# A new order of all steps, and products of zeros over 128 and over 64 rows, in a kernel of decay attention and mixture-of-experts attention

## The chip, the cores and the metric

The kernel runs on one core of a Trainium2 chip. The metric is the time of one execution on the device in microseconds (us), from the start of the program to its end; the median of three runs is given. The engines of the core are TensorE (PE; its loading of weights is shown apart as PEld), VectorE (DVE), ScalarE (ACT), GpSimd (POOL) and SyncE (SP), which here issues the transfers (DMA). Tiles in PSUM are where PE writes its products.

## The reference

There are 8 batches, 8 heads, 576 positions and a head dimension of 64. A causal attention with a decay comes first; its output, 512 columns wide, is the input of an attention with 4 experts, of which a gate picks two for each position.

```python
scores = scale * np.matmul(q, k.transpose(0, 1, 3, 2))
cum = np.cumsum(np.log(np.clip(f, 0.0001, 1.0)), axis=-1)
scores = np.where(causal, -1000000000.0, scores + cum[:, :, :, None] - cum[:, :, None, :])
attn = np.exp(scores - np.max(scores, axis=-1, keepdims=True))
x = np.matmul(attn / (np.sum(attn, axis=-1, keepdims=True) + 1e-09), v)
...
logits = x @ w_gate
topk = np.argpartition(-logits, 2, axis=-1)[..., :2]
w = softmax of the two chosen logits
for e in range(E):
    q, k, v = x @ wq[e], x @ wk[e], x @ wv[e]
    a = causal softmax of scale * (q @ k.transpose(0, 2, 1))
    out += (w of e, or zero where e is not chosen) * (a @ v @ wo[e])
```

## The kernel before

The work is cut into units of two heads: four for each batch in the first attention (a0_0 is batch 0, heads 0 and 1) and two of two experts each in the second (m0_0). A unit goes through a row of steps, each a Python generator that yields after nearly every instruction:

- prep_attn (L369) has SP fetch queries and keys into xin, ACT rounds them into kq (L377, twice: keys, queries), DVE subtracts to get the rest ka (L383, twice), and SP copies the bits of each into the other tile (L367). Rows with the running sums of the logarithms of the decay (chl) come into kq by way of a DRAM tile ex (L292 to L304, L363), for the first unit straight from chl (L359).
- max_pass (L532) has PE make products m0 to m3 in PSUM (L541), DVE adds the mask and takes maxima of them (mxs at L547, mxt at L560), PE turns the maxima around (mp, L604), ACT negates them (ms, L607), and SP writes them into a row of kq (L367), so that the products that follow have the maximum subtracted already. m and mp tiles share a pool of two tiles in PSUM.
- scores (L629) makes the products s0 to s3 (L638, L639); ACT takes their exponentials P, POOL clears what lies above the diagonal (L625, L658) and adds up rows (R, L701 to L707). attend (L713) multiplies by the values va (oa, ob, L726).
- For the experts, moe_front (L400) makes the values and the logits of a batch (pv, L417, in five blocks), copies the logits out (lg, L436) and works out the gate on DVE (L443 to L475: comparisons g and t of 128x80, wins, the largest logit mx, gt) with one exponential on ACT (L464). prep_moe (L497) makes queries and keys of the experts (pp, L513, twelve products for a tile), ACT rounds them (L521), DVE subtracts (ka_m, L523). project_out (L847) multiplies by wo and sends the output.

The order of all this is a table: ORDER (L27) is a string of two-digit numbers to base 64, each the number of a task, and each entry moves that task on by one yield. After that every instruction of an engine is made to follow the one written before it on the same engine (L920 to L925), so the order on each engine is fixed by the table; nothing overtakes, and an instruction that waits holds up all behind it on its engine.

PE begins with products of zeros: a tile wz of zeros (L179), multiplied with itself into a tile of PSUM that nobody reads. warm(8) at L271 issues eight at the front. In prep_attn of the first three units two more are issued with each of ACT's conversions (L379) and one with each of DVE's subtractions (L385), and each is made to wait for the instruction it is issued with.

## Time and profile before

| | |
|---|---|
| runs | 747.75, 748.61, 749.22 us; median 748.61 |
| profiled execution | 747.97 us, of which 746.2 are the span of the profile |
| mean clock granted to PE | 0.975 of full speed |
| PE, DVE, POOL, ACT busy | 694.5, 587.7, 453.6, 445.9 us |
| PE's share of the chain that ended last | 64%; DVE 21%, ACT 4%, issue 3%, DMA 3%, POOL 3% |

The page cuts the span into 40 slices of 18.7 us and gives for each the busy share of an engine and the clock that PE was granted, in tenths. PE runs at one of two clocks, 2.4 or 1.2 GHz, which the page shows as 1.0 and 0.5. A row of the timeline is one instruction or a run of like ones, with its start, its duration and, in brackets, how long the engine stood idle before it and on whose work it waited. Products overlap, so a row's duration is longer than the step to the next row. The profile times one execution; its clock records begin at 13.27 us, and the slice before shows full speed without one.

### The profile page before, as it was taken

The page shows a single profiled execution, that of the slowest core. Times are in us where ns is not written, and L with a number is a line of the kernel's source. Part 1 is how long each engine was busy: PE and PEld are TensorE (multiplying, and loading weights), DVE is VectorE, ACT ScalarE, POOL GpSimd, SP SyncE. Part 2 cuts the span into 40 slices and gives each one's busy share as a digit, 9 for nine tenths or more (in the row PEclk, how much of TensorE's full clock was granted, in tenths as well). Part 3 has the DMA queues.
Part 4 walks back from the last instruction along what each step waited for, and adds up shares of the span by engine and source line. Part 5 has one row for each costly group of instructions (what it writes and reads, how often), then busy time and mean ns, then how long its engine had stood idle before and what let it go on. Part 6 is the DMA issues. An engine that isn't in the chain of part 4 may idle for free.

```text
span 746.2 us, 15368 instructions
## 1 busy us (share of the span) xinstructions
PE 694.5 (93%) x5346; PEld 557.8 (75%) x5346; DVE 587.7 (79%) x1666; ACT 445.9 (60%) x959; POOL 453.6 (61%) x767
## 2 busy tenths in 40 slices
PE   5788899989999989999899999999899999999987
PEld 1455687768787778878797787878688777879754
DVE  7578987988879788888789788788978898765732
ACT  3566655666477655686466664766466664655443
POOL 8788774685475863673656745765645864535350
PEclk9599999999999999999999999999999999999989
DMA  7776333432324244345243426353252442213103
GB/s 166 187 162 149 92 87 82 124 81 64 104 74 126 67 101 118 96 123 120 63 120 96 114 52 145 87 139 89 61 136 68 129 94 52 52 49 76 32 5 124
DMA packets 29470, 72.82 MB, mean 98 GB/s; under 512 B 4169, under 2 KB 4649, under 8 KB 27345
## 3 DMA queue, kind: packets, MB, share of 16 engines
q1 hardware_dynamic: 29393, 71.84, 38.9%
q8 instruction: 42, 0.69, 0.4%
q14 instruction: 35, 0.29, 0.1%
HBM read 32.91 MB, written 10.35 MB: 58 GB/s over the span
## 4 chain that ended last, share of the span: by engine, by line
PE 64%; DVE 21%; ACT 4%; issue 3%; DMA 3%; POOL 3%; SPq 0%; DVEq 0%; ACTq 0%
PE pp_m L513 11%; PE pv L417 7%; PE s_a L638 6%; PE m_a L541 5%; PE po L859 5%; PE s_a L639 5%; PE ob_a L726 5%; DVE ka_a L383 4%; DVE junk_a L547 4%; PE s_m L638 3%; PE m_m L541 3%; PE s_m L639 3%; PE sm_a L766 2%; PE ob_m L726 2%; PE oa_a L726 2%
## 5 line engine op out<-in xcount | busy, mean ns | idle before, releaser
L547 DVE CUSTOM_DVE_ANT_0 junk_a<-m_a,mask 128x320 bf16<-128x320 f32 (+2 forms) x192 | 93.5, 487 | 29.3 <-PE m_a L541 19.3
L638 PE MATMUL s_a<-ka_a 128*128 128x320 f32 (+4 forms) x384 | 111.8, 315 | 1.9 <-ACT P_a L655 1.2
L541 PE MATMUL m_a<-kq 128*128 128x320 f32 (+4 forms) x384 | 95.9, 326 | 18.8 <-DVE mxs_a L547 8.3
L639 PE MATMUL s_a<-kq 128*128 128x320 f32 (+4 forms) x384 | 104.6, 300 | 1.2 <-DMA kq<-ms_a 1.1
L383 DVE TENSOR_TENSOR ka_a<-xin,kq 64x1152 fp32r<-64x1152 f32 x64 | 98.1, 1533 | 2.7 <-ACT kq L377 1.3
L625 POOL TENSOR_SCALAR_AFFINE_SELECT P_a<-P_a 128x128 f32<-128x128 f32 x128 | 39.6, 312 | 94.4 <-ACT P_a L673 51.9
L521 ACT ACTIVATE kq<-pp_m 64x288 fp32r<-64x288 f32 x128 | 51.8, 405 | 67.0 <-DVE ka_m L523 42.3
L541 PEld LDWEIGHTS m_a<-kq 128*128 128x128 f32 (+1 forms) x384 | 64.0, 188 | 35.5 <-DVE mxs_a L547 16.2
L523 DVE TENSOR_TENSOR ka_m<-pp_m,kq 64x288 fp32r<-64x288 f32 x128 | 58.2, 454 | 38.9 <-ACT kq L521 36.4
L638 PEld LDWEIGHTS s_a<-ka_a 128*128 128x128 f32 (+1 forms) x384 | 71.0, 185 | 13.5 <-ACT P_a L655 3.8
L377 ACT ACTIVATE kq<-xin 64x1152 fp32r<-64x1152 f32 x64 | 72.5, 1157 | 8.9 <-DMA xin<-in_qk_dram 8.1
L701 POOL TENSOR_TENSOR R_a<-P_a 128x448 f32<-128x448 f32 x64 | 76.8, 1200 | 0.0
L658 POOL TENSOR_SCALAR_AFFINE_SELECT P_a<-P_a 128x256 f32<-128x256 f32 x64 | 31.8, 503 | 70.0 <-ACT P_a L655 69.7
L639 PEld LDWEIGHTS s_a<-kq 128*128 128x128 f32 (+1 forms) x384 | 70.5, 185 | 2.6 <-DMA kq<-ms_a 1.9
L726 PE MATMUL ob_a<-P_a,va 128*64 128x320 f32 (+1 forms) x512 | 67.7, 407 | 0.0
L703 POOL TENSOR_TENSOR R_a<-R_a,P_a 128x320 f32<-128x320 f32 x64 | 65.0, 1016 | 4.3
L638 PE MATMUL s_m<-ka_m 128*128 128x192 f32 (+2 forms) x192 | 56.0, 315 | 2.0 <-ACT P_m L655 1.6
L547 DVE CUSTOM_DVE_ANT_0 junk_m<-m_m,mask 128x192 bf16<-128x192 f32 (+2 forms) x96 | 46.6, 485 | 10.9 <-PE m_m L541 7.0
L726 PEld LDWEIGHTS ob_a<-P_a,va 128*64 128x64 f32 x512 | 35.9, 138 | 24.1 <-issue 0.2
L655 ACT ACTIVATE P_a<-s_a 128x512 f32<-128x512 f32 x64 | 37.2, 596 | 25.9 <-PE s_a L639 24.9
L639 PE MATMUL s_m<-kq 128*128 128x192 f32 (+2 forms) x192 | 52.2, 299 | 0.4 <-DMA kq<-ms_m 0.3
L673 ACT ACTIVATE P_a<-s_a 128x448 f32<-128x448 f32 x64 | 34.5, 545 | 25.6 <-PE s_a L639 25.0
(189 smaller groups left out, 2057.2 us busy)
## 6 DMA issues: line engine op xcount, KB each, us to landing
xin<-in_qk_dram SPq DMA_DIRECT2D x32, 576.0 KB
ka_a<-kq SPq DMA_DIRECT2D x64, 288.0 KB
va<-in_v_dram SPq DMA_DIRECT2D x32, 320.0 KB
ka_m<-kq SPq DMA_DIRECT2D x32, 288.0 KB
out_dram<-outb SPq DMA_DIRECT2D x32, 256.0 KB
kq<-ex SPq DMA_DIRECT2D x47, 27.0 KB
kq<-ms_a SPq DMA_DIRECT2D x64, 2.5 KB
out_dram<-outb SPq DMA_DIRECT2D x8, 128.0 KB
```

The source lines that it names most:

```text
L377: made = nc.scalar.activation(hi[near], x[:, 2 * c : 2 * c + 2], AF.Copy)
L383: made = nc.vector.tensor_tensor(lo, x[:, 2 * c : 2 * c + 2], hi[near].bitcast(F32), ALU.subtract)
L417: nc.tensor.matmul(pv[:, :NV], l[c][:, t0 : t0 + 128], r[:, c], start=(n == 0), stop=(n == 3 * KC - 1))
L513: nc.tensor.matmul(pp[:, :HS], w[:, c, es], x[c][:, gs], start=(n == 0), stop=(n == 3 * KC - 1))
L523: nc.vector.tensor_tensor(lo[:, h, gs], src, hv.bitcast(F32), ALU.subtract)
L541: nc.tensor.matmul(dst, qB[0:K, h, i0 : i0 + dst.shape[0]], kB[0:K, h, j0:j1], start=True, stop=True)
L547: nc.vector.tensor_tensor_reduce(jk[:, :n], src, mask[:, MW - n :], 1.0, init, ALU.add, ALU.max, acc)
L638: nc.tensor.matmul(dst, kaf[:, c : c + m], qA[:, h, i0:i1], start=True, stop=False)
L639: nc.tensor.matmul(dst, kqf[0:K, c + h * S : c + h * S + m], qB[0:K, h, i0:i1], start=False, stop=True)
L701: g.tensor_tensor(r[:, h, 128:S], q[:, 320:768], q[:, 768:1216], ALU.add)
L703: g.tensor_tensor(r[:, h, 256:S], r[:, h, 256:S], q[:, 1216:1536], ALU.add)
L726: mm = nc.tensor.matmul(dst[64 * h : 64 * h + 64, c0 : c0 + rhs.shape[-1]], vs[h][0:kp, blk], rhs, start=first, stop=last,)
```

## The change

The zeros change in kind. wz is now float32 of 128x512 in place of bfloat16, its memset accordingly twice as large, and there are two tiles of PSUM for the products. warm(at, cols, ...) issues one product for each start row in `at`: (0,) is one over all 128 rows (or over the lower 64), (0, 64) a pair of products over 64 rows each, into the two tiles. At the front there are 3 over 128 rows, 4 pairs, 3 over the lower half, 6 pairs of only 128 columns, and three times one over 128 rows and a pair: 23 products of 512 columns and 12 of 128, where there were 8. In the first three units a conversion has a pair with it (before: two products), a subtraction one product (as before).

ORDER is written anew from the first row to the last; its rows tell a reader nothing, so the diff shows one of each. Every instruction but the zeros is the same in kind and number.

```diff
 ORDER = """
-4w004w4w4w4w054x4z4x00004w4w000000004x4x4x4x02024x4y4y4y0202020202020202054x4x02020202024x4x4x4x4x4x4x4x4x074x0c
...
+4w4w4w4z004z02054x4w4w4w4y00004x4x00000000000202024x4x4x4x024x0202024y4y0505004y0c020202074x024y02024x4x4x054x4x
...
 """
 WARM = (1, 1, 1)
-WARM0 = 8
 
 
 @with_exitstack
@@ -176,14 +175,15 @@
     NKQ = 4
     kqs = [const.tile([128, 2, 2, S], F32R, name=f"kq{i}") for i in range(NKQ)]
     xin = const.tile([128, 4, S], F32, name="xin")
-    wz = const.tile([128, 512], BF16, name="wz")
-    nc.vector.memset(wz, 0.0)
-    wps = ptile(ps_o, "o", "warm")
-
-    def warm(n, after=None):
-
-        for _ in range(n):
-            mm = nc.tensor.matmul(wps, wz[:, 0:128], wz, start=True, stop=True)
+    wz = const.tile([128, 512], F32R, name="wz")
+    nc.vector.memset(wz.bitcast(F32), 0.0)
+    wps = [ptile(ps_o, "o", f"warm{i}") for i in range(2)]
+
+    def warm(at, cols, after=None, n=None):
+
+        for i, r in enumerate(at):
+            k = slice(r, r + (n or 128 // len(at)))
+            mm = nc.tensor.matmul(wps[i][:, :cols], wz[k, 0:128], wz[k, :cols], start=True, stop=True)
             if after is not None:
                 together(mm, after)
 
@@ -268,7 +268,10 @@
     neg = rows.tile([128, 2, S], F32, tag="R", name="neg")[:NR]
     nc.vector.memset(neg, -1.0)
 
-    warm(WARM0)
+    full, halves_, low_half = ((0,), 512), ((0, 64), 512), ((0,), 512, None, 64)
+    thin = ((0, 64), 128)
+    for args in 3 * [full] + 4 * [halves_] + 3 * [low_half] + 6 * [thin] + 3 * [full, halves_]:
+        warm(*args)
 
     def decay_rows():
         cum = prob.tile([128, 2, 1536], F32, tag="P", name="cum")[:NR, 0, :S]
@@ -376,13 +379,15 @@
         for c, hi in ((1, kB), (0, qB)):
             made = nc.scalar.activation(hi[near], x[:, 2 * c : 2 * c + 2], AF.Copy)
             if u["first"] is not None:
-                warm(2 * WARM[u["first"]], made)
+                for _ in range(WARM[u["first"]]):
+                    warm((0, 64), 512, made)
             yield
         yield from extra_rows(u, b * NPH + hp)
         for c, hi, lo in ((1, kB, kA[far]), (0, qB, qA[near])):
             made = nc.vector.tensor_tensor(lo, x[:, 2 * c : 2 * c + 2], hi[near].bitcast(F32), ALU.subtract)
             if u["first"] is not None:
-                warm(WARM[u["first"]], made)
+                for _ in range(WARM[u["first"]]):
+                    warm((0,), 512, made)
             yield
         copy_bits(kA[near], kB[near])
         yield
```

What moves is shown at three places, by the rows of an engine in the order of the program (a number at the end of a name is the number of the tile; three dots mark rows left out; line numbers of the changed kernel are up to five higher).

SP's queue at its start, before. xin is the transfer of queries and keys of a unit (the third is that of a0_2), chl the decay rows, ka_a0_0 the rest of the first unit's queries and keys:

```order
L374 DMA xin_112<-in_qk_dram 64x2304 x2
L337 DMA st_v0_152<-in_wv_dram 128x512
L359 DMA kq0_108<-chl_122 2x1x576 x2
L292 DMA ex_119<-chl_122 64x2x576
L294 DMA ex_119<-neg_126 64x2x576
L296 DMA ex_119<-one_123 64x1152
L374 DMA xin_112<-in_qk_dram 64x2304
...
L367 DMA ka_a0_0_138<-kq0_108 64x2x576
...
L367 DMA ka_a0_0_138<-kq0_108 64x2x576
```

And SP's queue at the same place, changed:

```order
L340 DMA st_v0_170<-in_wv_dram 128x512
L377 DMA xin_112<-in_qk_dram 64x2304 x2
L295 DMA ex_120<-chl_123 64x2x576
L362 DMA kq0_108<-chl_123 2x1x576 x2
L370 DMA ka_a0_0_172<-kq0_108 64x2x576
L297 DMA ex_120<-neg_127 64x2x576
L299 DMA ex_120<-one_124 64x1152
L370 DMA ka_a0_0_172<-kq0_108 64x2x576
L377 DMA xin_112<-in_qk_dram 64x2304
```

The write of chl to ex is now ahead of the two copies of chl into kq0, both copies of ka_a0_0 are ahead of the third xin, and the other weights, before between the third xin and ka_a0_0, follow later.

PE at the fifth gate, before, from the last product of pv5_4 (which holds the logits) to the second pair of m0 products of a6_3, for which PE waited; m0_a6_3, mp_a6_2 and m3_a6_2 share the pool of two tiles:

```order
L417 MATMUL pv5_4_7306<-vh_150,xl_a5_2_1_6947 128x260
L513 MATMUL pp_m5_0_7319<-xh_a5_2_0_6805,kh_273 128x288
...
L541 MATMUL m0_a6_3_7353<-kq1_109 128x192
L541 MATMUL m0_a6_3_7353<-kq1_109 128x320
L726 MATMUL oa_a6_1_7358<-P_a6_1_7189,va1_102 64x256 x2
...
L726 MATMUL ob_a6_1_7360<-pl2_107,va1_102 64x64 x2
L604 MATMUL mp_a6_2_7387<-ident_90,mxs_a6_2_7034 10x128
L513 MATMUL pp_m5_0_7407<-xh_a5_0_0_6485,kh_273 128x288
L513 MATMUL pp_m5_0_7407<-xl_a5_0_0_6486,kh_273 128x288
L513 MATMUL pp_m5_0_7407<-xh_a5_0_0_6485,kl_274 128x288
L541 MATMUL m0_a6_3_7411<-kq1_109 128x192
```

And PE at the same place, changed; between the rows shown there are 24 pp products in all and the two blocks of s3_a6_1:

```order
L422 MATMUL pv5_4_7320<-vh_168,xl_a5_2_1_6988 128x260
L546 MATMUL m3_a6_2_7337<-kq0_108 128x320
L518 MATMUL pp_m5_0_7348<-xh_a5_0_0_6495,kh_335 128x288
...
L643 MATMUL s3_a6_1_7369<-ka_a6_1_6526 128x320
...
L609 MATMUL mp_a6_2_7378<-ident_90,mxs_a6_2_7110 10x128
L546 MATMUL m0_a6_3_7409<-kq1_109 128x192
L518 MATMUL pp_m5_0_7416<-xh_a5_0_0_6495,kh_335 128x288
...
L731 MATMUL oa_a6_1_7430<-P_a6_1_7219,va1_102 64x256 x2
...
L546 MATMUL m0_a6_3_7449<-kq1_109 128x192
```

Before, 6 + 3 pp products, one pair of m0, the attend products (oa, ob) and mp stand between the last pv product and the second pair of m0. Now it is the last m3, 24 pp, s3, mp, one pair of m0 and the attend products, and mp stands ahead of the first m0 instead of between the two.

DVE at the fifth gate, before, with the last reduction of a6_2 (junk_a6_2) and the first of a6_3:

```order
L547 ISA junk_a6_2_7317,mxs_a6_2_7034<-m3_a6_2_7313,mask_95 128x320
L843 TENSOR_TENSOR yl_m4_0_1_7276<-ot_m4_1_6965,yh_m4_0_1_7275 128x512
L436 COPY lg5_7079<-pv5_4_7306 128x4
L443 TENSOR_TENSOR g45_7347<-lg5_7079 128x80
L445 TENSOR_TENSOR t45_7348<-lg5_7079 128x80
...
L462 TENSOR_TENSOR gt5_7382<-lg5_7079,mx5_7380 128x20
L547 ISA junk_a6_3_7384,mxs_a6_3_7350<-m0_a6_3_7353,mask_95 128x192
L560 TENSOR_REDUCE mxt_a6_3_7352<-m0_a6_3_7353 128x1
L523 TENSOR_TENSOR ka_m5_0_7218<-pp_m5_0_7319,kq2_110 64x288 x2
```

And DVE at the same place, changed:

```order
L441 COPY lg5_7096<-pv5_4_7320 128x4
L448 TENSOR_TENSOR g45_7341<-lg5_7096 128x80
L552 ISA junk_a6_2_7346,mxs_a6_2_7110<-m3_a6_2_7337,mask_95 128x320
L848 TENSOR_TENSOR yl_m4_0_1_7313<-ot_m4_1_7006,yh_m4_0_1_7312 128x512
L450 TENSOR_TENSOR t45_7342<-lg5_7096 128x80
...
L467 TENSOR_TENSOR gt5_7403<-lg5_7096,mx5_7401 128x20
L528 TENSOR_TENSOR ka_m5_0_7178<-pp_m5_0_7348,kq2_110 64x288 x2
L552 ISA junk_a6_3_7412,mxs_a6_3_7352<-m0_a6_3_7409,mask_95 128x192
```

The last reduction of a6_2 and the subtraction yl now stand inside the gate, and two ka_m subtractions between the gate and the first reduction of a6_3. PE and DVE are changed in a like manner at the gates of the other batches. On PE the m3 products of the first unit stand ahead of the zeros that are issued with the third unit's conversions, and on SP the load of va2 stands behind the maxima of a0_2 (kq2<-ms_a0_2), where it stood ahead.

## Rows read from the trace of the kernel before

**Rows 1.** the slices of the page: TensorE's granted clock, in tenths of full speed

```profile
PEclk9599999999999999999999999999999999999989
```

**Rows 2.** busy time by stretch: window, length, busy us (instructions) of each engine, clock

```profile
core 0: us, PE busy (x) PEld busy (x) DVE busy (x) ACT busy (x) POOL busy (x), PEclk, DMA share, GB/s
0.00:60.00 60.00, 42.15 (x189) 25.33 (x189) 40.94 (x92) 30.17 (x50) 48.40 (x76) 0.80 0.77 174
400.00:600.00 200.00, 193.18 (x1506) 158.38 (x1505) 166.98 (x476) 127.54 (x273) 127.28 (x213) 0.99 0.42 104
```

**Rows 3.** timeline of PE: start, us, what (count), in brackets idle time before it

```profile
1.26 3.59 PE L186 MATMUL warm<-wz 128*128 128x512 bf16 x8 [1.26 <-DVE wz L180]
9.33 2.52 PE L186 MATMUL warm<-wz 128*128 128x512 bf16 x5 [4.48 <-ACT kq L377]
```

**Rows 4.** timeline of DVE at the start

```profile
0.94 0.27 DVE L180 MEMSET wz<- 128x256 uint32 x1 [0.94 <-PEq L952]
23.44 0.49 DVE L547 CUSTOM_DVE_ANT_0 junk_a<-m_a,mask 128x320 bf16<-128x320 f32 x1 [2.92 <-PE m_a L541]
```

**Rows 5.** timeline of SP's queue, at its issues, over the first 56 us

```profile
10.51 0.68 SPq L292 DMA_DIRECT2D ex<-chl  x1
19.66 0.66 SPq L367 DMA_DIRECT2D ka_a<-kq  x1
21.50 0.82 SPq L367 DMA_DIRECT2D ka_a<-kq  x1
46.78 1.27 SPq L395 DMA_DIRECT2D va<-in_v_dram  x1
```

**Rows 6.** the chain that ended last: start, us, transfer

```profile
51.77 5.55 DMA kq<-ms_a
334.61 3.07 DMA kq<-ms_a
```

**Rows 7.** timeline of PE: what waits behind the gate of each batch

```profile
194.50 0.28 PE L604 MATMUL mp_a<-ident,mxs_a 128*10 128x128 f32 x1 [1.34 <-DVE mxs_a L547]
279.78 0.28 PE L604 MATMUL mp_a<-ident,mxs_a 128*10 128x128 f32 x1 [2.13 <-DVE mxs_a L547]
367.00 0.37 PE L513 MATMUL pp_m<-xh_a,qh 128*128 128x288 f32 x1 [2.16 <-DVE ka_m L523]
454.28 0.39 PE L541 MATMUL m_a<-kq 128*128 128x256 f32 x1 [0.90 <-DVE mxt_a L560]
538.17 0.52 PE L541 MATMUL m_a<-kq 128*128 128x192 f32 x2 [2.87 <-DVE mxt_a L560]
626.91 0.39 PE L541 MATMUL m_a<-kq 128*128 128x256 f32 x1 [1.46 <-DVE mxs_a L547]
```

**Rows 8.** busy time by stretch: two stretches behind a gate, columns as above

```profile
368.26:371.67 3.41, 3.41 (x16) 3.12 (x14) 1.74 (x6) 1.88 (x5) 0.12 (x1) 0.50 0.76 159
538.93:542.33 3.40, 3.40 (x17) 3.40 (x16) 2.38 (x9) 1.63 (x5) 0.00 (x0) 0.50 0.02 5
```

**Rows 9.** timeline of PE ahead of the wait at 538.17

```profile
530.52 0.28 PE L417 MATMUL pv<-vh,xl_a 128*128 128x260 f32 x1
530.63 0.29 PE L513 MATMUL pp_m<-xh_a,kh 128*128 128x288 f32 x1
531.77 0.87 PE L726 MATMUL oa_a<-P_a,va 128*64 128x256 f32 x8
```

**Rows 10.** timeline of DVE beside it, the fifth gate

```profile
530.76 1.99 DVE L843 TENSOR_TENSOR yl_m<-ot_m,yh_m 128x512 fp32r<-128x512 f32 x1
532.68 0.15 DVE L436 COPY lg<-pv 128x4 f32<-128x4 f32 x1
537.01 0.42 DVE L462 TENSOR_TENSOR gt<-lg,mx 128x20 f32<-128x20 f32 x1
```

**Rows 11.** PE's waits by line: for what, us, times, longest

```profile
PE m_a L541 <- DVE mxs_a L547: 8.3, 13, 1.5
```

**Rows 12.** one line of the gate: ns shortest, middle, longest, first and last start

```profile
L447 DVE TENSOR_TENSOR g<-g,up x8: 229/628/1580, 122.0 to 707.3; 128x80 f32<-128x80 f32 x8
```

188 lines of the change are left out of this document (94 added, 94 removed).

## The prediction

> **What bounds the kernel now.** I read the slices of the page first, then busy time by stretch, then what TensorE (PE) waited for, then the queue of SyncE (SP) and the other engines where a wait pointed at them. In the middle of the kernel PE is the bound: it is busy for 193.18 of the 200 us from 400 to 600, at a granted clock of 0.99 of full speed, while VectorE (DVE) has 166.98 and ScalarE and GpSimd less than 130 each [rows 2]. An order of work can win there only the idle 3.4%, and whatever time the clock is lowered. In the first 60 us PE is busy for 42.15 and so idle for 17.85, with a mean clock of 0.80 [rows 2]; the second slice of the span stands at half speed (a 5, the level of 1.2 GHz) [rows 1]. So there are two places to look at: the start, and the few large waits of the middle.
>
> The large waits of the middle stand where DVE works out the gate of the mixture of experts, once for each batch. In batches 1 to 6 there are six, at 194.50, 279.78, 367.00, 454.28, 538.17 and 626.91: 1.34 + 2.13 + 2.16 + 0.90 + 2.87 + 1.46 = 10.86 us in all [rows 7]. Two of them, those of 2.16 and 2.87, are followed by a stretch of 3.41 and 3.40 us in which the granted clock is 0.50, PE being busy throughout [rows 8]; what ran at half speed for 3.4 us takes 1.7 at full speed, so each of these stretches costs 1.7. The reader is to see that PE fell to the lower level right after it had stood still for over 2 us, and that the 2.13 us at 279.78 were not followed by such a stretch.
>
> **The zeros at the front.** PE first runs eight products of zeros in 3.59 us, 0.449 each, and then waits 4.48 us for the first conversion of the queries and keys [rows 3]. The changed kernel puts 16 such lengths there if the two products of a pair run beside each other, with six thin pairs of a quarter of the columns: 16 x 0.449 + 6 x 0.11 = 7.8 us; one after the other it is 23 lengths and 12 thin ones, 11.7 us. Before there was 3.59 + 4.48 = 8.07 us. The first fits into the wait and costs nothing; the second would push the zeros 3.6 us past it, of which the later products of zeros (they wait for ACT and DVE in any case) take up some. Bounds 0 and +3; I take 0, since a thing that fits into a wait of 4.48 us is the nearer row. No row of this trace has a product over 64 rows in two banks. The Trainium skill ("TensorEngine Tiling (Array Packing)", Key Properties) says that tiles work independently, so that pairs would run beside each other, but also that a change of the tiling mode, not merely of the tile, drains TensorE; that speaks against a list that alternates between full products and pairs. By the first half of it the sum is the one taken, by the second a drain is added at each of the dozen changes, and no run here gives its price.
>
> **The start behind them.** The memset of zeros is twice as large: 0.27 us [rows 4] becomes an estimated 0.54, and DVE's chain to the decay rows starts 0.27 later. On SP's queue the write of the decay rows to DRAM (0.68, [rows 5]) now stands ahead of the two copies that the first unit needs, and the two copies of ka_a0_0 stand ahead of the third transfer of xin. These two take 0.66 + 0.82 = 1.48 us of the queue [rows 5]. In the kernel before, what held the first unit up was that the second m3 product and the products behind it stood behind zeros tied to the third unit's conversion, which waited for that transfer of xin: DVE stood idle for 2.92 us until it came, at 23.44 [rows 4]. The m3 products are now ahead of these zeros, so the 2.92 go. What is late next is still the third xin, now 1.48 us later in its queue, since the conversion's zeros remain ahead of mp_a0_0. Net 2.92 - 1.48 = 1.44, and the copies of ka_a0_0, which the first scores need, are no longer behind the weights: I take -1.6. Bounds -2.9 (the later xin is hidden) and +1.5 (it is not, and the 2.92 comes back).
>
> A second place: the rows of maxima of a0_2 reached kq2 by a transfer that took 5.55 us on the chain, against 3.07 for the same transfer at 334.61 [rows 6]. Ahead of it in the queue stood the load of va2, 1.27 us of issue [rows 5]; this now stands behind. I take -1.3; bounds 0 and -2.5 (the difference of the two rows). The start is worth -2.9 in sum. That the half-speed stretch at the start goes as well is not counted; it would be worth up to 4 us, since the second slice of 18.7 us holds at most some 8 us of products that could run at double the speed [rows 1].
>
> **The gates.** Take the fifth. The last product of pv starts at 530.52 [rows 9]. Then PE has, before, six pp products and two m0 products (530.63 to 531.77: 1.14 us), and the attend products, mp and three pp (531.77 to the start of the wait at 538.17 - 2.87 = 535.30: 3.53 us): 4.67 us of work [rows 7, 9]. DVE in the same time finishes a subtraction of 1.99 us, starts the gate at 532.68 and ends its last operation at 537.43, 4.75 us later, and only then reduces m0, for which PE waits [rows 10]. In the changed order PE has behind the last pv product: one m3, 24 pp, two blocks of scores, mp, two m0 and the attend products. By the same rows a pp is 0.13 us, so this is 3.2 + 0.2 + 0.8 + 0.35 + 2.9 = about 7.4 us ahead of the second pair of m0. DVE's chain has grown by the last m3 reduction (0.57) and two ka_m subtractions (0.95): 4.75 + 0.57 + 0.95 plus the same subtraction, 0.7 at its shortest and 1.99 here, is 7.0 to 8.3 us. The counts at the other five gates come to 6.7 to 7.5 us of PE's work, where it was 3.6 to 5.8. What is left of a wait is between nothing and 1.6 us; I take 0.9, a little above the middle, which is also the smallest of the six rows. That leaves 6 x 0.9 = 5.4 of 10.86, or -5.5. Bounds 0 (the waits stay) and -10.9. As none of the waits then reaches 2.16, the two stretches at half speed go too: -3.4. The middle: -8.9.
>
> **What is given back.** Everything else in the table is permuted by a place or two, and the same engines' work has to fit together anew. PE waited 13 times, 8.3 us, for a maximum that DVE had not yet reduced, 0.64 each [rows 11]. Where the work under a transfer of maxima has become shorter (a0_0, a1_1, m1_1, m3_1, a6_1), and at the gates where the m reductions now stand behind ka_m, I count six new waits of 0.6: +3.6. Bounds 0 and 8.3.
>
> **Sum.** The profiled execution took 747.97 us, of which 746.2 are the span; the median of the runs is 0.64 above it. -2.9 - 8.9 + 3.6 = -8.2, so 739.8 for a profiled execution and **740.4** for the median.
>
> **Rivals.** *The chain on DVE grows with its cover* (slower). The gate's operations have two operands in SBUF and run while GpSimd adds up rows: the same multiplication of 128x80 took between 0.229 and 1.580 us over the eight batches, 0.628 in the middle [rows 12]. More of GpSimd's sums may now fall on the gate. From 2.2 us more than the 8.3, which is two operations at their longest, the waits are at 10.9 or more in sum as before, each above 2 us, and the clock falls behind all six instead of two: 6 x 1.7 - 3.4 = +6.8; with the start (-2.9) and what is given back (+3.6) that is +7.5, some 756. For it: the spread of that row. Against it: it needs the longest form at most of the six. The Trainium skill ("SBUF — State Buffer", SBUF: two separate sides) has the pair of ports that DVE and GpSimd share as an exclusive lock, held for the whole instruction, which a DVE operation with two SBUF inputs takes against a GpSimd operation that reads SBUF; the spread of the row agrees. *No change*: PE's cover is longer but DVE had never been idle there, so that the waits only move to the next product, and the two stretches at half speed stay: -2.9 + 3.6 = +0.7, about 749. *A larger gain*: the gate waits vanish (-10.9 - 3.4), nothing is given back and the start brings 2.9: 731; with the clock held at the start 727. *The zeros don't hold the clock and only lengthen the front*: +3 on the forecast, inside its range.
>
> **Chances.** The forecast, 734 to 746.9, 0.60; the larger gain 0.10; no change 0.14; slower 0.16. The range of 731 to 750.5 takes in the forecast, no change and half of the larger gain. What a measurement of this kernel can tell from no change is about 0.2%, 1.5 us: faster by more 0.70, within 0.14, slower by more 0.16.
>
> **What would show it.** In the profile after: the six waits behind the gate at 0.9 or less in place of 0.90 to 2.87, with m0 or pp of the next half as the waiting product; no row at a clock of 0.50 between 60 and 700 us; PE busy for more than 195 of the 200 us from 400 to 600; the first mp before 25 us; a transfer of maxima to kq2 of 3 to 4.3 us. The forecast is wrong if the gate's operations on DVE span over 6 us beside GpSimd's sums, if waits over 2 us appear at other products, or if the zeros last beyond the first conversion.

## The result: 26 us faster, three times what was forecast

The changed kernel took 721.71 us in the median (720.00 to 722.83, four runs), the kernel before beside it 748.18 (747.57 to 749.22): a ratio of 0.9643, with an interval of 0.962 to 0.9666, or 26.5 us less. The forecast was 740.4 with a range of 731 to 750.5; it had the sign, and the time lies 9 us below the range. The profiled execution took 721.82 us, of which 719.9 are the span; all that follows compares this span with the 746.2 of before.

The page of the changed kernel, busy time of each engine and the slices that answer to [rows 1]:

```profile
PE 687.3 (95%) x5373; PEld 559.8 (78%) x5373; DVE 575.9 (80%) x1666; ACT 445.2 (62%) x959; POOL 469.3 (65%) x767
...
PE   8788899999999999999999999999999999999997
...
PEclk9588999999999999999999999999999999999999
```

The clock of the start is much what it was: a half-clock slice and two more that are not whole. From the sixth slice on PE is at 9 to the last but one. On the chain that ended last DVE has 9% where it had 21, and GpSimd 10% where it had 3. The same windows as [rows 2], in the changed kernel (window, length, busy us and instructions of PE, PEld, DVE, ACT and POOL, granted clock, DMA share, GB/s):

```profile
0.00:60.00 60.00, 49.39 (x229) 32.98 (x233) 41.05 (x94) 30.00 (x51) 51.24 (x77) 0.80 0.71 173
400.00:600.00 200.00, 196.45 (x1594) 164.64 (x1591) 169.48 (x498) 132.04 (x282) 135.37 (x218) 1.00 0.44 107
```

The 49.39 us of PE in the first 60 hold the longer list of zeros. In 400 to 600 PE is busy for 196.45 of the 200 us in place of 193.18. That is 3.3 us less idle time, and alone would be some 9 us over the whole middle; a later piece of the program lies in the window now, so a comparison needs cuts at the same products.

I cut both executions at these: the last one of pv0_4, the first of pv7_0 and the last of pv7_4 (pv are the values and logits of a batch). The experts and gates of batches 1 to 6 lie in the second stretch.

| stretch | before, us | after, us | difference | forecast |
|---|---|---|---|---|
| start to pv0_4 | 119.92 | 118.49 | -1.4 | -2.9 |
| pv0_4 to pv7_0, "the middle" | 565.24 | 545.25 | -20.0 | -8.9 + 3.6 = -5.3 |
| pv7_0 to pv7_4 | 20.4 | 19.3 | -1.1 | 0 |
| pv7_4 to the end, "the tail" | 40.7 | 36.9 | -3.8 | 0 |
| span | 746.2 | 719.9 | -26.3 | -8.2 |

The rows of the middle and the tail, first of the kernel before, then of the changed one (columns as above):

```profile
119.92:685.16 565.24, 543.45 (x4360) 448.95 (x4358) 467.06 (x1350) 353.73 (x769) 342.00 (x585) 0.99 0.37 93
705.53:746.20 40.67, 33.52 (x221) 22.25 (x219) 15.14 (x42) 16.41 (x39) 14.29 (x23) 0.92 0.17 59
```

```profile
118.49:663.74 545.25, 533.50 (x4362) 445.52 (x4360) 455.72 (x1344) 353.77 (x770) 357.32 (x590) 1.00 0.40 98
683.00:719.90 36.90, 30.68 (x221) 20.39 (x219) 16.64 (x41) 16.48 (x39) 14.64 (x23) 1.00 0.20 72
```

The same 4,360 or so products fill the middle of both. PE's idle time there, length less busy time, went from 21.79 to 11.75 us: 10.0 of the 20.0. The two stretches at half clock [rows 8] are gone: 3.4 more. What is left, 6.55, lies inside the busy time. What PE waited for in 119 to 690 us, before (line, released by, us in all, times, longest):

```profile
PE mp_a L604 <- DVE mxs_a L547: 3.9, 3, 2.1
PE m_a L541 <- DVE mxt_a L560: 3.8, 2, 2.9
PE m_a L541 <- DVE mxs_a L547: 3.3, 5, 1.5
PE pp_m L513 <- DVE ka_m L523: 2.2, 1, 2.2
```

and in the changed kernel, the largest:

```profile
PE m_a L546 <- DVE mxs_a L552: 2.5, 5, 0.6
PE sm_m L771 <- POOL R_m L712: 1.5, 3, 0.7
PE s_m L644 <- DMA kq<-ms_m: 1.5, 1, 1.5
```

All six waits of [rows 7] are gone; no wait behind a gate is over 0.7 us. The fifth gate shows how. DVE there, in the changed kernel (start, us, line and operation, in brackets idle time before it):

```profile
517.85 0.16 DVE L441 COPY lg<-pv 128x4 f32<-128x4 f32 x1
...
518.62 0.69 DVE L848 TENSOR_TENSOR yl_m<-ot_m,yh_m 128x512 fp32r<-128x512 f32 x1
...
519.47 0.23 DVE L452 TENSOR_TENSOR g<-g,up 128x80 f32<-128x80 f32 x1
...
520.44 1.25 DVE L461 TENSOR_SCALAR wins<-wins 128x20 f32<-128x20 f32 x1
...
521.80 0.83 DVE L467 TENSOR_TENSOR gt<-lg,mx 128x20 f32<-128x20 f32 x1
...
523.59 0.46 DVE L528 TENSOR_TENSOR ka_m<-pp_m,kq 64x288 fp32r<-64x288 f32 x1 [0.47 <-ACT kq L526]
```

beside GpSimd's first sum of the stretch, in the changed kernel and then in the one before, where the gate began at 532.87:

```profile
520.51 1.14 POOL L706 TENSOR_TENSOR R_a<-P_a 128x448 f32<-128x448 f32 x1
```

```profile
531.07 1.13 POOL L701 TENSOR_TENSOR R_a<-P_a 128x448 f32<-128x448 f32 x1
```

and PE, from the first product behind pv to the queries of the next half:

```profile
516.70 0.31 PE L546 MATMUL m_a<-kq 128*128 128x320 f32 x1
...
524.14 0.52 PE L546 MATMUL m_a<-kq 128*128 128x192 f32 x2
524.50 0.29 PE L518 MATMUL pp_m<-xh_a,qh 128*128 128x288 f32 x1
```

PE has 7.44 us of work between 516.70 and 524.14 and no wait in it; forecast was 7.4. DVE's subtraction yl takes 0.69 where it took 1.99 [rows 10], and g times up 0.23 where it took 0.62 to 1.58 in several batches [rows 12]. GpSimd's sums now begin behind the middle of the gate, and it is there that single operations are long (1.25, 0.83). I added up the nine operations of each gate, from g to gt, over batches 1 to 6: 3.78 + 4.44 + 5.09 + 3.10 + 4.75 + 3.81 = 24.97 us before, 2.75 + 2.04 + 4.04 + 2.96 + 3.75 + 1.97 = 17.5 after. In the two gates with no sum beside them, batches 2 and 6, it is 2.0 each; beside the others 2.0 to 5.3 us of sums run.

### The profile page after: what moved, and what is told of

The parts are those of the page before. It is cut to its first block, busy times and chain, and to the rows that moved or that the text cites. A ratio compares the mean times of both kernels' runs of the same rounds, so it can differ in the third digit from the quotient of the medians.

```text
span 719.9 us, 15408 instructions
## 1 busy us (share of the span) xinstructions
PE 687.3 (95%) x5373; PEld 559.8 (78%) x5373; DVE 575.9 (80%) x1666; ACT 445.2 (62%) x959; POOL 469.3 (65%) x767
## 4 chain that ended last, share of the span: by engine, by line
PE 68%; POOL 10%; DVE 9%; ACT 5%; DMA 4%; issue 3%; SPq 0%; POOLq 0%; DVEq 0%; ACTq 0%
PE pp_m L518 10%; PE pv L422 7%; PE ob_a L731 6%; PE s_a L643 6%; PE m_a L546 5%; PE po L864 5%; PE s_a L644 5%; PE s_m L643 4%; PE m_m L546 3%; PE s_m L644 3%; PE oa_a L731 3%; POOL R_m L706 3%; PE sm_a L771 2%; PE warm L186 2%; POOL R_m L708 2%
## 5 line engine op out<-in xcount | busy, mean ns | idle before, releaser
L630 POOL TENSOR_SCALAR_AFFINE_SELECT P_a<-P_a 128x128 f32<-128x128 f32 x128 | 45.9, 361 | 107.0 <-ACT P_a L693 59.6
L546 PE MATMUL m_a<-kq 128*128 128x320 f32 (+4 forms) x384 | 93.4, 316 | 7.2 <-DVE mxs_a L552 4.0
L387 DVE TENSOR_TENSOR ka_a<-xin,kq 64x1152 fp32r<-64x1152 f32 x64 | 96.2, 1503 | 2.5 <-ACT kq L380 1.0
L706 POOL TENSOR_TENSOR R_a<-P_a 128x448 f32<-128x448 f32 x64 | 78.7, 1230 | 0.0
L731 PE MATMUL ob_a<-P_a,va 128*64 128x320 f32 (+1 forms) x512 | 68.8, 411 | 0.0
L630 POOL TENSOR_SCALAR_AFFINE_SELECT P_m<-P_m 128x128 f32<-128x128 f32 x64 | 19.7, 310 | 44.4 <-ACT P_m L678 29.8
```

Of the source, the lines that this page charges most:

```text
L387: made = nc.vector.tensor_tensor(lo, x[:, 2 * c : 2 * c + 2], hi[near].bitcast(F32), ALU.subtract)
L546: nc.tensor.matmul(dst, qB[0:K, h, i0 : i0 + dst.shape[0]], kB[0:K, h, j0:j1], start=True, stop=True)
L630: return nc.gpsimd.affine_select(pv, pv, [[1, 128]], ALU.is_ge, 0.0, base=0, channel_multiplier=-1)
L706: g.tensor_tensor(r[:, h, 128:S], q[:, 320:768], q[:, 768:1216], ALU.add)
L731: mm = nc.tensor.matmul(dst[64 * h : 64 * h + 64, c0 : c0 + rhs.shape[-1]], vs[h][0:kp, blk], rhs, start=first, stop=last,)
```

## Experiments

The theory after the result: the gates were slow because GpSimd's sums ran beside them, the new table moves the sums and the gate apart and puts more of PE's work over it, and that is most of the 20 us. The rivals: the gain is the cover alone; or it comes from the permutation of everything between the gates; or from the zeros, the start or the clock. In diffs of the table only the first row that differs stands; the number of entries, of 5,285, is told. Differences in us are the ratio's, times 748.

### One part of the change at a time

**The six gates alone**: in the kernel before, entries 1112 to 1290 and five like stretches (some 60 entries ahead of each gate to 70 behind it) in the order of the changed table.

```diff
-0-0-0-180V0V0V0-0-0-0V0V0-0U0U0-0-0V130V0-13131a1d13130-0-1k1k131k1k0V1k0-1k1k1k1k1k0-0-0-0V1a1a1313131k1k1k1k1k
+0-0-0-180V0V0V0-0-0-0V0V0-0U0U0-0-0V130V0-13131a1d13130-0-1k1k131k1k0V1k0-1k1k1k1k1k0-0-0-0V1a1a0a1313131313180-
...
```

> The kernel before, zeros and all, with the entries of six stretches of the table (one around each gate of batches 1 to 6, some 1160 of 5285 entries) put in the order that they have in the changed table; everything else stays. Theory A, the gates carry the gain by themselves: the six waits (10.86 us) and the two stretches at half clock (3.4 us) go, 748.2 - 14.3 = about 734. Theory B, my forecast's step: 0.9 of each wait stays and other waits take some back, 748.2 - 5.5 - 3.4 + 3.6 = 743. Theory C, the waits only move to the next product since VectorE was never idle there: 747 to 749.

Measured: 737.92 us, ratio 0.989 (0.9859 to 0.9922), or -8.2. The gate operations take 17.5 us in sum, as in the changed kernel, and the six waits are gone, but PE's idle time in the middle falls only from 21.8 to 16.4:

```profile
119.04:676.27 557.23, 540.85 (x4360) 446.80 (x4358) 458.18 (x1350) 353.22 (x769) 345.10 (x585) 1.00 0.38 95
129.40:132.80 3.40, 3.40 (x16) 3.36 (x16) 2.37 (x9) 2.63 (x5) 0.81 (x2) 0.50 0.85 268
```

New waits have come, among them products of row sums (sm) behind two of the gates that wait for DVE, and one stretch at half clock in another place. PE of this kernel:

```profile
201.82 0.69 PE L766 MATMUL sm_a<-R_a,ones_col 128*32 128x288 f32 x8 [1.27 <-DVE gt L466]
```

```profile
370.58 0.69 PE L766 MATMUL sm_a<-R_a,ones_col 128*32 128x288 f32 x8 [1.38 <-DVE ka_m L523]
```

GpSimd's last sum had ended at 199.4, well before the first of these; DVE, which ended both, was still at the subtractions and the last multiplication behind the gate. The wait has moved along DVE's queue. So of 10.9 us of waits 5.4 were won and 5.5 given back. That is not far from the forecast of the middle (-5.3 with what is given back), but by other terms: 5.5 us of waits were to go and 10.9 went, 3.6 were to come back and 5.5 came, and one of the two half-clock stretches is still there. That the sums lie close is in part luck. How the 8 us divide between the shorter gate on DVE and the longer cover on PE, no run separates.

**The gates undone**: the changed kernel with its six stretches in the old order.

```diff
-1k1k1k1k1k1k13130V1k1k1k1d1a1a1k0-0W0W1a1l0-1414141414140-0-1k1k1a0W0W18181d1d1a1a100W0W1a1a1a0t1a1k0W0W0W0W0W1a
+1k1k0d0F0S0Y1k1k1a0V0W0W1k1k13131d1d1a0W0W1k101k0W1k1a0-1a10101d1k0-1k1k0-0-0W0W14141k0W0W0W1a0W1a14141d14141k14
...
```

> The changed kernel with the entries of the six stretches around the gates put back in the order that they have in the table before. Theory A: the waits behind the gates come back, and with those over 2 us a lower clock, 721.7 + 14.3 = about 736. Theory B: 721.7 + 9 = about 730. If the rest of the table has made slack there (earlier maxima, fewer sums of GpSimd beside the gate), less than 726.

Measured: 736.64, ratio 0.9872 (0.9842 to 0.9902): 15 us more than the changed kernel by the medians, 17 by the ratios. Waits of 1.33, 2.11, 2.16, 2.23 and 0.83 us are back behind the gates. The gates are worth 8 us in the old table and 15 to 17 in the new one.

**The new zeros alone**, with the old table:

```diff
+    for args in 3 * [full] + 4 * [halves_] + 3 * [low_half] + 6 * [thin] + 3 * [full, halves_]:
+        warm(*args)
```

> The kernel before with the new products of zeros (kinds, number, larger memset), the table unchanged. My forecast: they fit into TensorE's first wait of 4.48 us, 748.2 within 1 us. Theory that pairs run one after the other: 12 us of zeros at the front, +2 to +4 us. Theory that they hold the clock in the first 40 us: -2 to -4 us.

Measured: 749.08, ratio 1.003 (1.0006 to 1.0054), or +2.2; its profiled execution shows nothing of that up to pv0_4 (119.82 for 119.92). **The new table alone**, with the old zeros (the reverse of it):

```diff
-    for args in 3 * [full] + 4 * [halves_] + 3 * [low_half] + 6 * [thin] + 3 * [full, halves_]:
-        warm(*args)
+    warm(WARM0)
```

> The changed table with the zeros of the kernel before. If the new zeros do nothing, as forecast: 721.7 within 1 us. If they keep the clock up in the start of the changed table: 2 to 4 us more. If they only lengthen the front (they cost 1.1 us with the old table): 720.5.

Measured: 721.29, ratio 0.9618 (0.9582 to 0.9654). The table is the whole gain; the zeros add nothing to it.

**The first 520 entries, the entries 520 to 4950, and those behind 4950**, one at a time. The first goes with the new zeros, the other two with the old.

```diff
-4w004w4w4w4w054x4z4x00004w4w000000004x4x4x4x02024x4y4y4y0202020202020202054x4x02020202024x4x4x4x4x4x4x4x4x074x0c
+4w4w4w4z004z02054x4w4w4w4y00004x4x00000000000202024x4x4x4x024x0202024y4y0505004y0c020202074x024y02024x4x4x054x4x
...
```

> The kernel before with the new zeros and with the first 520 entries of the table (about the first 80 us) in the order that they have in the changed table. My forecast for the start: 748 - 2.9 = 745. If the start is held by the transfers as before and the zeros cost what they cost alone: 748 to 749. If it brings what the changed kernel is ahead at its first product of the values, with the zeros' work taken off: 748 - 1 = 747.

```diff
-0s0n0v0v0v0u0A0F0n0n0w0w0w0n0w0C0C0C0C0n0n0n0r0n0r0n0p0n0w0w0w0w0n0N0C0C0C0C4z0w0w0w0w0w0w0n0M0M0w0w0w0w0C0w0C0n
+0s0n0v0v0v0u0A0F0n0n0w0w0w0n0w0C4z0a0g0r0n0C0w0w0C0C0w0n0n0n0n0n0C0C0C0C0w0Y0n0w0w0w0B0w0C0M0M0M0C0w0w0n0w0w0w0w
...
```

> The kernel before, with its zeros, start and tail, and the entries 520 to 4950 of the table (about 80 to 680 us) in the order of the changed table. Between pv0_4 and pv7_0 the changed kernel takes 545.2 us where the kernel before took 565.3. If the middle's gain is its own: 748 - 20 = about 728. If part of it needs the start or the tail: 732 to 736. The gates alone gave 738.

```diff
-3S4p4p4m4p4m4p4p4p4p4p4p4p4p4p4p4f4f4f4f4k4p4f4f4m4f4p4f4m4f4f4f4f4m4f4c4f4m4k4k4k4k4k4k4k4k4k4k4k4k4k4k4m4m2O4m
+3S4p4p4m4p4m4p4p4p4p4p4p4p4p4p4p4f4f4f4f4k4p3i3y3x3m3W3J46423I4c464f4f4f4f4f4f4f4m4m4m4f4f4m4f4p4k4k4m4k4k4k4m4k
...
```

> The kernel before with the last 335 entries of its table (about from 680 us on) put in the order that they have in the changed table. Between the last product of the values (pv7_4) and the end the changed kernel is 3.7 us shorter. If the order of the tail alone does that (a wait of 1.60 us at 711.65 goes, and the 6.8 us at half clock behind it): 748.2 - 4 = about 744. If it comes from what stands ahead (work that had already been done by then): 747 to 748.

Measured: start 743.18, ratio 0.993 (0.9902 to 0.9957), -5.2; middle 728.13, ratio 0.9703 (0.9662 to 0.9745), -22.2; tail 744.97, ratio 0.9963 (0.9943 to 0.9983), -2.8. In sum -30, against -26.7 for the whole by its ratio, which the intervals allow. The middle of "middle" is that of the changed kernel:

```profile
119.72:664.01 544.29, 532.93 (x4360) 445.24 (x4358) 457.72 (x1344) 353.67 (x769) 355.21 (x587) 1.00 0.40 98
```

The tail's row, in the kernel with the new tail alone:

```profile
708.30:745.20 36.90, 30.69 (x221) 20.39 (x219) 16.62 (x41) 16.45 (x39) 14.62 (x23) 0.98 0.21 72
```

It is 36.9 us as in the changed kernel. Before, scores of the last unit waited 1.60 us and a stretch of half clock followed, so that the clock of the 40.67 us was 0.92; now that wait is 0.92 us. PE's row and the stretch, in the kernel before:

```profile
711.65 0.39 PE L638 MATMUL s_m<-ka_m 128*128 128x256 f32 x1 [1.60 <-ACT P_m L655]
```

```profile
713.01:719.83 6.82, 6.75 (x59) 4.90 (x61) 2.26 (x7) 3.86 (x11) 3.87 (x9) 0.50 0.00 0
```

The length of the tail has the clock's part in it: with the new zeros and the old tail it took 37.8 us in that execution, with no fall of the clock, so the order alone shows 0.9 there. For the start the profile shows less than the ratio: pv0_4 is only 0.9 us earlier (119.06), and the rest appears later, where the wait at the fifth gate is 1.84 us and not 2.87 and no half clock follows it.

**All of 520 to 4950 but the six stretches**:

```diff
-0s0n0v0v0v0u0A0F0n0n0w0w0w0n0w0C0C0C0C0n0n0n0r0n0r0n0p0n0w0w0w0w0n0N0C0C0C0C4z0w0w0w0w0w0w0n0M0M0w0w0w0w0C0w0C0n
+0s0n0v0v0v0u0A0F0n0n0w0w0w0n0w0C4z0r0n0C0w0w0C0C0w0n0n0n0n0n0C0C0C0C0w0Y0n0w0w0w0B0w0C0M0M0M0C0w0w0n0w0w0w0w0w0w
...
```

> The kernel before with the entries 520 to 4950 in the order of the changed table, but for the six stretches around the gates, which keep theirs. The middle as a whole gave 21 us, the six stretches alone 10. If the two add up: 748 - 11 = 737. If the rest of the order is only worth something where the gates are laid anew: 744 to 748.

Measured: 746.04, ratio 0.9975 (0.9952 to 0.9998), or -1.9. PE's idle time in the middle is 564.73 - 542.11 = 22.6 us, no less than before, and the gate waits stay (1.34, 2.19, 2.17, 0.90, 1.82, 0.86):

```profile
121.84:686.57 564.73, 542.11 (x4359) 451.43 (x4358) 465.14 (x1344) 355.35 (x769) 349.02 (x587) 0.99 0.37 94
```

So the middle is 8 from the gates, 2 from what lies between them, and some 12, give or take 4, that come only when both are there. The profiled executions say what kind of time that is. For the middle of each, in us: its length, PE's idle time, what of it ran at half clock, and the count of pauses, steps between products outside the half-clock stretches that are over 0.04 us longer than the columns take at 2.4 GHz:

| middle of | length | idle | at half clock | pauses |
|---|---|---|---|---|
| before | 565.2 | 21.8 | 6.8 | 960 |
| the six gates alone | 557.2 | 16.4 | 3.4 | 936 |
| all but the gates | 564.7 | 22.6 | 13.7 | 897 |
| changed | 545.3 | 11.8 | 0 | 880 |

The entries between the gates do bring most of the fewer pauses by themselves (63 of 80; the stretches left out may hide some ten). In this execution that was lost again to four stretches at half clock, three of them behind gate waits that still stand; one of the four:

```profile
543.52:546.93 3.41, 3.41 (x17) 3.41 (x16) 2.56 (x9) 1.40 (x4) 0.00 (x0) 0.50 0.02 5
```

What comes only with both is 5.4 us of idle time and, at half of each stretch, some 5 of clock. The clock's part belongs to the executions profiled: this one took 749.27 us, the slowest of ten from 742.01 on. To learn on which side of the gates these 12 lie, I made the six stretches **longer by 100 entries behind, and by 100 ahead**:

```diff
-0-0-0-180V0V0V0-0-0-0V0V0-0U0U0-0-0V130V0-13131a1d13130-0-1k1k131k1k0V1k0-1k1k1k1k1k0-0-0-0V1a1a1313131k1k1k1k1k
+0-0-0-180V0V0V0-0-0-0V0V0-0U0U0-0-0V130V0-13131a1d13130-0-1k1k131k1k0V1k0-1k1k1k1k1k0-0-0-0V1a1a0a0m0x1313131313
...
```

> The kernel before with the six stretches around the gates in the order of the changed table, each longer by 100 entries at its end (1694 entries in all, where the run with the gates alone had 1094), so that they take in the row sums' products behind the gate. With the gates alone products of row sums waited 1.27 and 1.38 us and a fall of the clock came once more. If the gates need what stands behind them: 748 - 15 to -19, 729 to 733. If they need what stands ahead: 737 to 739, as with the gates alone.

```diff
-0+0+0+0+0T0T0T0T0T0T0L0T0T130T0Y0T0T0T0Q120T0T0+0+0+0Q0+13130L0L0L0L13131313130+0L0U0-0-0-0-13131313130-0-0-1d0-
+0+0+0+0+0a1d0T0T0T0T0T0T0T0T0T0T0T0T0T120T0+0Q0Q130+0+13130L0L0+0L0+0L13130L13130U130L1313130-13130-0-0-0-0-130-
...
```

> The same, but each stretch longer by 100 entries at its beginning instead. If the gates need what stands ahead of them (maxima and sums done before the gate): 729 to 733. If they need what stands behind: 737 to 739. If both are below 735, the gain is spread over the whole order and neither side carries it.

Measured: 738.40, ratio 0.9866 (0.9816 to 0.9916), and 741.31, ratio 0.9893 (0.9848 to 0.9939). Neither brings more than the gates alone. The second has a new wait, at the joint of the two orders:

```profile
258.89 0.53 PE L639 MATMUL s_a<-kq 128*128 128x192 f32 x1 [5.45 <-DMA kq<-ms_a]
```

A stretch of 6.83 us at half clock begins in it:

```profile
257.69:264.52 6.83, 5.63 (x25) 4.53 (x29) 2.75 (x6) 2.42 (x5) 0.82 (x4) 0.50 0.15 57
```

Wait and clock are some 8 us, made by the cut; less them the run would stand near 733, the edge of what was expected if the gates need what lies ahead. So the second run doesn't exclude that side, and it has fewer pauses (909, where the first has 937 and the gates alone 936). The first does speak against the side behind: the waits of 1.27 and 1.38 us at the row sums are gone in it, and PE's idle time in the middle is 16.4 us all the same.

### GpSimd's sums beside the gates

**The sums taken away** in the old table:

```diff
+        quiet = u["kind"] == "a" and u["p"] < 2 and u["b"] >= 2
         for h in range(2):
             q = p[:, h]
-            g.tensor_tensor(r[:, h, 128:S], q[:, 320:768], q[:, 768:1216], ALU.add)
+            if quiet:
+                g.memset(r[:, h, 128:S], 1.0)
+            else:
+                g.tensor_tensor(r[:, h, 128:S], q[:, 320:768], q[:, 768:1216], ALU.add)
...
```

> The kernel before, table unchanged; for the first two units of each batch from a2 on GpSimd writes ones into the row sums (memset, which reads nothing) in place of adding rows up, so nothing of GpSimd reads SBUF beside the gates of batches 1 to 6. This leaves the row sums of these units out. Theory P, the gate's chain on VectorE is long because its operations stand against GpSimd's sums: the nine operations of the six gates, 24.97 us together before, come down to about 6 x 1.95 = 11.7, the six waits of 10.86 us shrink by some 8, and the two falls of the clock (3.4) go: 748 - 11 = about 737. Theory Q, it is TensorE's cover alone that matters: the operations stay as long, 747 to 748.

Measured: 729.92, ratio 0.9743 (0.9699 to 0.9787), or -19.2. The nine operations take 12.7 us in sum, 1.9 to 2.2 at each gate but the first (2.5), no gate wait is left, and the clock doesn't fall in the middle:

```profile
121.00:668.57 547.57, 538.10 (x4360) 445.61 (x4358) 447.43 (x1350) 353.44 (x769) 295.96 (x585) 1.00 0.39 96
```

PE's idle time there is 9.5 us, with the old order and the old cover. This is what these sums cost the kernel before, through DVE and by coming late. It is a bound for the gates and not their price, since the sums of two units in each batch are gone wherever they ran, and DVE's busy time in the middle falls by 19.6 us, of which the gates are 12.3. Nor is GpSimd silent there: it still clears P and writes the ones. **The same in the changed kernel**:

```diff
+        quiet = u["kind"] == "a" and u["p"] < 2 and u["b"] >= 2
...
-            g.tensor_tensor(r[:, h, 128:S], q[:, 320:768], q[:, 768:1216], ALU.add)
+            if quiet:
+                g.memset(r[:, h, 128:S], 1.0)
...
```

> The changed kernel with ones written in place of GpSimd's sums for the first two units of each batch from a2 on, which leaves their row sums out. Theory P: the changed order already keeps the sums off the gate or covers them, so little is left: 721 to 717. If GpSimd's sums cost as much anywhere: 721 - 19 = 702.

Measured: 718.49, ratio 0.9614 (0.9585 to 0.9642), 2 to 3 us below the changed kernel, where the same edit gave 19 in the old one. In the new table little is left of what these sums cost.

**The sums held back**: nothing left out, but in the old table each sum that ran beside a gate waits for the gate's last operation, its entries moved behind it.

```diff
+    gated = {}
+    HOLD = {(2, 0, 1): 1, (2, 1, 0): 1, (3, 1, 0): 2, (4, 0, 1): 3, (4, 1, 0): 3, (5, 1, 0): 4, (6, 0, 1): 5, (6, 1, 0): 5, (7, 1, 0): 6}
...
-            g.tensor_tensor(r[:, h, 128:S], q[:, 320:768], q[:, 768:1216], ALU.add)
+            add = g.tensor_tensor(r[:, h, 128:S], q[:, 320:768], q[:, 768:1216], ALU.add)
+            if u["kind"] == "a" and (u["b"], u["p"], h) in HOLD:
+                together(add, gated[HOLD[u["b"], u["p"], h]])
```

> The kernel before with one thing held back: in batches 1 to 6 GpSimd's sums that ran beside the gate wait for the gate's last operation with two operands (gt, L462) on VectorE; nothing is left out. Theory P (the sums lengthen the gate): the gate's nine operations come down to about 2 us in each of the six batches, the waits of 10.86 us shrink by most of their size, and what GpSimd is late by is covered, since it idles over 6 us behind the gate: 748 - 9 to -17, about 735. If it was freeing GpSimd altogether that helped when the sums were left out, and not the gate: 748 or slower, since the sums now end up to 3 us later.

Measured: 752.00, ratio 1.0049 (1.0022 to 1.0076), or +3.7. The gate operations take 2.0 us at every gate and the gate waits are gone, and yet it is slower. What PE waits for in 119 to 690 us of this kernel:

```profile
PE sm_a L770 <- POOL R_a L711: 8.7, 5, 4.6
PE oa_a L730 <- POOL pl L697: 3.0, 1, 3.0
```

and one of the five:

```profile
633.63 1.67 PE L770 MATMUL sm_a<-R_a,ones_col 128*32 128x288 f32 x12 [4.55 <-POOL R_a L711]
```

The row sums are late by what GpSimd was held back, and the products sm that use them stand where they stood. The contention is cured and paid for at the next consumer. In the changed table these products stand later: for batches 3 and 6, PE is busy for 11.7 and 12.0 us between the last pv and the first of them, where it is for 9.4 and 9.1 here. **The same wait in the changed table**:

```diff
+    HOLD = {(2, 1, 0): 1, (3, 1, 0): 2, (4, 1, 0): 3, (5, 1, 0): 4, (6, 1, 0): 5, (7, 1, 0): 6}
...
+                together(add, gated[HOLD[u["b"], u["p"], h]])
```

> The changed kernel with the sums of the second unit of each batch from a2 on held until the gate's last operation with two operands. Theory P: the gates of batches 1, 3, 4 and 5 get some 0.8 to 2 us shorter on VectorE, but no product waits there any more: 719 to 722. If the held sums are needed sooner in this order: 722 to 726.

Measured: 722.20, ratio 0.9654 (0.9616 to 0.9692): no gain, within what the changed kernel takes.

### The zeros

**The changed kernel once more, without the zeros issued with the conversions, and without any**, on one chip:

> The changed kernel once more, to stand beside the next two on the same chip: 720 to 723.

```diff
-            if u["first"] is not None:
-                for _ in range(WARM[u["first"]]):
-                    warm((0, 64), 512, made)
...
```

> The changed kernel without the zeros that are issued with the conversions and subtractions of the first three units; those at the front stay. If these zeros only hold products back (2.7 us wait for VectorE at 19.7 us): 1 to 2 us faster, 720. If they keep the clock from falling for longer: 2 to 4 us slower, 725.

```diff
-    wz = const.tile([128, 512], F32R, name="wz")
-    nc.vector.memset(wz.bitcast(F32), 0.0)
...
-    for args in 3 * [full] + 4 * [halves_] + 3 * [low_half] + 6 * [thin] + 3 * [full, halves_]:
-        warm(*args)
...
```

> The changed kernel without any products of zeros. If they hold no clock: as front_zeros or a little faster (no memset ahead of VectorE's chain, 0.5 us), 719.5 to 721. If the zeros at the front are what lifts the clock for the first products: the first 20 us at half speed, 3 to 5 us slower, 725.

Measured: 720.33 (ratio 0.962, 0.9593 to 0.9648), 719.71 (0.9599, 0.9578 to 0.962) and 719.27 (0.9592, 0.9571 to 0.9613). The three can't be told apart. The second shows the zeros of the front by themselves, on PE, and the changed kernel all up to its first product m0:

```profile
1.53 7.85 PE L186 MATMUL warm<-wz 128*128 128x512 f32 x35 [1.53 <-DVE wz L179]
```

```profile
1.53 12.45 PE L186 MATMUL warm<-wz 128*128 128x512 f32 x41 [1.53 <-DVE wz L179]
```

35 products in 7.85 us, where the forecast had 7.8 for pairs beside each other and 11.7 one after the other. But the 7.85 are not the forecast's 7.8. The clock of that execution was at full from 5.69 us, so the last six lengths ran at 2.4 GHz. In the changed kernel's profiled execution the clock records begin at 14.18, the products before run at the pace of 1.2 GHz (0.43 us for 512 columns), and the 35 take 10.2 us, until 11.8. Its rows, two pairs and then a full product, a pair and a full product:

```profile
3.70 0.63 PE L186 MATMUL warm<-wz 64*128 64x512 f32 x2
4.13 0.63 PE L186 MATMUL warm<-wz 64*128 64x512 f32 x2
...
7.56 0.79 PE L186 MATMUL warm<-wz 128*128 128x512 f32 x1
8.29 0.79 PE L186 MATMUL warm<-wz 64*128 64x512 f32 x2
9.01 0.79 PE L186 MATMUL warm<-wz 128*128 128x512 f32 x1
```

From pair to pair it is 0.43 us, no more than one product takes, so the two run beside each other; from one kind to the other it is 0.73. The zeros and those of the conversions follow each other without a break, and the first m0 product starts at 13.77 (before, 12.20).

Without zeros the first mp comes 2.5 us earlier, at 23.67 in place of 26.13, but the attend products at 40 us still run at half speed, 16 of them in 3.44 us, where the same 16 take 2.11 at 41.52 in the changed kernel. PE without any zeros:

```profile
23.67 0.39 PE L598 MATMUL mp_a<-ident,mxs_a 128*10 128x128 f32 x1
...
39.99 3.44 PE L720 MATMUL ob_a<-P_a,va 128*64 128x320 f32 x16
```

With the zeros the records of the granted clock show full speed from 14.18 to 17.59 us in the changed kernel, half until 38.07 and full again; without any they begin at 42.67, at full. So the zeros bring the clock back earlier and the first work later, and the times say only that the two come out about even.

## Why the prediction was wrong, and where it was right

**The place was right, the sum of the middle was not.** The gates were named, and the two views that led there, the waits of [rows 7] and the half-clock stretches of [rows 8], did hold the first half of the gain: 10.0 us less idle time and 3.4 of clock in the middle. Most tests of the middle came true: no gate wait over 0.9, no other wait over 2 us, 196.45 of 200 us in 400 to 600; and the cover of 7.4 at the fifth gate is 7.44. The test of the clock from 60 to 700 us failed by one stretch, at 65.4 to 68.8. Two of the signs of a wrong forecast came up: the operations of the gate of batch 3 span 6.4 us, and the zeros outlast the first conversion. In the terms of the sum, in us:

| term | forecast | measured |
|---|---|---|
| the start, to pv0_4 | -2.9 | -1.4 |
| waits at the gates | -5.5 | -10.9 |
| half clock behind them | -3.4 | -3.4 |
| given back as other idle time | +3.6 | +0.8 |
| products closer together, within PE's busy time | no term | -6.5 |
| pv7_0 to pv7_4 | no term | -1.1 |
| the tail | no term | -3.8 |
| span | -8.2 | -26.3 |

The 0.8 is what the 10.0 us less of idle time leave of 10.9. The clock's term came out, its reason did not: no wait was to reach 2.16 us, but a fall came behind one of 1.24 (in the kernel with the gates alone, at 129.41) and none behind one of 2.16 (in that with the gates undone).

**The step that failed first: "DVE's chain ... 7.0 to 8.3 us" and "what is left of a wait ... I take 0.9".** The chain was built from durations of [rows 10] that contained GpSimd's sums, and taken over as if these would stay where they were. GpSimd's order at the gates did not enter it: s3, on which the last clearing and the sums of a6_1 hang, had moved behind pv, so the sums begin late in the gate (520.51, before 531.07 with the gate from 532.87). The rows show 24.97 us of gate operations become 17.5, and yl 1.99 become 0.69; at the fifth gate the chain, from the logits at 517.85 to the end of the second ka_m at 524.05, took 6.2 us, less than the cover, and nothing is left of the wait. The rival "the chain on DVE grows" had the right mechanism and the wrong sign. Of it the Trainium skill ("SBUF — State Buffer", Who interferes with whom) says that a DVE instruction with two SBUF inputs contends with a GpSimd instruction that reads SBUF; the traces agree: the nine operations take 1.9 to 2.2 us (once 2.5) where no sum runs beside them, in "quiet", "guard" and the changed kernel, and up to 5.1 where one does. That the pair of ports is what they contend for, no run here shows. That rival's sum does not come out either: a chain of 8.3 + 2.2 us against 7.4 of cover leaves 3.1 at each gate, 18.6 in all and not 10.9.

**The second: "+3.6 given back".** In the old table it is too small: the gates alone gave back 5.5 us of waits. In the new table only 0.8 are given back, and more is won. "Everything else in the table is permuted by a place or two" was costed as a loss only; the entries between the gates bring 2 us alone and let the gates bring 15 to 17 instead of 8. Why, is shown only in kind (idle time and clock, in the table of the middles). That the products of row sums stand further back explains where the waits of "gates" (1.27 and 1.38 us) and "guard" (8.7 us) went, not the gain: "gates_wide" moves them back too and is no faster. By size: from "gates" to the changed kernel the middle loses 12.0 us, 4.6 of idle time, 1.7 of the half-clock stretch at 129.4, and 5.65 inside PE's busy time.

**What stays open** is that last part, 6.55 us of the 20.0 between before and after, for which the prediction had no term. In it the same products stand closer: there are 80 fewer pauses of about 0.1 us between products, about 30 of them between two products of scores. Most of them come with the entries between the gates alone. In 33 of them the product had just been released by another engine, DVE for the most part (2.4 us in all); what makes the rest was not found. Open too is which entries between the gates make the joint gain.

**The tail was left out.** It was put at nothing without a reason, and took 2.8 us off as a single part (3.8 in the profile, of which some 2.9 are the clock). The wait of 1.60 at 711.65 and the clock of 0.92 behind it stood in the trace of before, in the same form as the gates' (the page's slices show the 8 at the end, [rows 1]).

**The start was half wrong.** For the first mp -1.6 was taken; it came at 26.13 in place of 26.37, and not before 25. The third xin was issued at 15.17 and not 12.80, behind both copies of ka_a0_0, and ACT got to the conversions only then:

```profile
22.49 2.22 ACT L380 ACTIVATE kq<-xin 64x1152 fp32r<-64x1152 f32 x2 [9.65 <-DMA xin<-in_qk_dram]
```

In the kernel before they began at 19.66. So the later xin was not 1.48 us but 2.8, which eats the 2.92 of [rows 4]: the net was named as the right one and its second term was too small. The transfer of maxima of a0_2 [rows 6] is no longer on the chain, and the wait for it at 57.37 us (0.67) is gone, as forecast; to pv0_4 both together are -1.4 of -2.9 (-2.6 in the profiled execution of "after_again", the same kernel). How much of the start is worth in the median (-5.2 as a part alone, 0.9 of it visible in its profile) is not settled.

**The zeros at nothing were right in the time, not in the reason.** With them or without, the changed table takes the same within its spread. But they do not fit into the wait of 4.48 us: at half clock the 35 take 10.2 us for 7.8 and end at 11.8, over 2 us behind the first conversion (DVE's subtraction, which needs it, starts at 9.58), and DVE's first reduction comes at 14.54 in place of 13.34. What the sum lacked is the change of kind, 0.73 us from a full product to a pair or back where it took 0.449, and the thin pairs, which took twice their 0.11. That this costs nothing in the end is luck of the start: mp waits there for the third unit's conversion in any case. The Trainium skill ("TensorEngine Tiling (Array Packing)", Key Properties) has independent tiles and a drain of TensorE at each change of the tiling mode; the trace agrees with both, by the 0.43 us from pair to pair and the 0.3 more at a change, though that it is a drain no row shows.

**The range** left out the large gain because its case was priced at most at 14.3 us in the middle and 2.9 at the start. The waits that a view of waits lists were the whole of that bound; 6.55 us lay in pauses too short to be listed, and 3.8 in the tail.
